# First chunk of a fused attention and two-FFN kernel: the sign of a weight piece ahead of its successor's rebase, head and rest one tick later, and the 1e-9 behind the exponentials

## Chip, core and metric

The kernel runs on one NeuronCore of one Trainium2 chip, in one launch. The metric is the device time in microseconds (us). TensorE is called PE in the profile, VectorE DVE, ScalarE ACT, GpSimd POOL, SyncE SP.

## What is computed

Three stages, each fed by the one before. Attention with 4 batches, 8 heads, 576 positions and head size 64; half of the heads see the last 32 positions, the other half every 32nd one. Then an FFN with h - tanh(h), then a gated FFN with silu. Everything is in fp32.

```python
scores = scale * np.matmul(q, k.transpose(0, 1, 3, 2))
scores = np.where(masks[None, :, :, :], scores, -1000000000.0)
scores = scores - np.max(scores, axis=-1, keepdims=True)
attn = np.exp(scores)
attn = attn / (np.sum(attn, axis=-1, keepdims=True) + 1e-09)
x = np.matmul(attn, v)                      # to (2304, 512)
h = x @ w_in                                # 512 -> 2048
x = (h - np.tanh(h)) @ w_out                # 2048 -> 512
g = x @ w_gate                              # 512 -> 1536
silu = g * (1.0 / (1.0 + np.exp(-g)))
out = silu * (x @ w_val) @ w_out2
```

## The kernel before

To keep fp32 precision, each matmul is made three times (`mm3`, L189 to L193) from operands that are split in two: a rounded high part and the remainder. So every weight must be split too. A weight comes in pieces of 128x512, read as 64-bit words, and a piece goes through eight steps (class `Piece`, L110 to L157):

- `load`: DMA from SyncE's queue into a staging buffer `st` (five of them, shared by all pieces)
- `high` (ScalarE, L124): the upper words without sign into a tile `m` (four tiles, used in turn); `low` (ScalarE, L127): the lower words scaled, in place
- `clamp` (VectorE, L130) and `shift` (VectorE, L134), together `rebase`: on `m`
- `join` (GpSimd, L142): adds the lower words to `m`
- `sign` (VectorE, L146): brings the sign from `st` into `m`; after it `st` is free
- `head` (ScalarE, L152): the rounded part of `m` into the weight tile `w`
- `rest` (GpSimd, L155): the remainder into `w`; `m` is free again. For eight of the 32 pieces, the streamed ones, `then` follows: a DMA from SyncE's queue that stores `w` for the later chunks.

The tokens are worked in five chunks. In the first one (c = 0, 512 tokens) the 32 weight pieces are made as they are needed. The first four are made during the attention of batch 0; the other 28 in the loop over f = 0 to 15 (16 slices of the hidden layer), two per iteration, by two calls of `feed1.tick()`. A tick is a stage of a pipeline over the pieces: tick t loads ahead, begins piece t, and goes on with the pieces begun in the ticks before it.

One iteration f of this loop issues, in this order: GpSimd's normalisation of the scores of attention group f-1 (`norm`: 1e-9 added on ScalarE at L290, reciprocal on VectorE at L294, multiplication on GpSimd at L296); the first part on TensorE (`first_part`, 12 matmuls into `ps_h`); tanh on ScalarE (L520) and h - tanh(h) on VectorE (L521); TensorE's product of group f-3 with the values; the first tick; TensorE's scores of group f (L265) and their masked maximum on VectorE (`top`, L273); the second part of f-1 on TensorE (12 matmuls into `ps_acc`); the transposes of group f-1 (L308) and their copy on VectorE (`bring`, L312); the split of the result (`parts`: L527 on ScalarE, L528 on VectorE); the exponentials of group f on ScalarE (L282), which also sum the rows; the second tick. There are twelve groups, so f = 13 to 15 have no scores and no normalisation. The first six groups are 80 columns wide (240 elements in the multiplication), the last six 96 (288).

Each engine works off its instructions in the order in which they are issued, and waits on semaphores for the others. There is no planner in this part: the order of the lines is the order on every engine. The first part at f needs piece 2f-1, the second part of f-1 needs piece 2f. From the second chunk on, the pieces are all there.

BV is 2. Batch 0's attention runs ahead of the loop; batch b = 1 runs in the first chunk, b = 2 and 3 in later ones.

Of the kernel before, what the change touches and what calls it, by code (L numbers as in the profile page):

```python
# [13 lines left out]
AF = mybir.ActivationFunctionType  # L14
# [19 lines left out]
BV = 2  # L34
# [39 lines left out]
def model_kernel(ctx: ExitStack, tc: tile.TileContext, q, k, v, mask, ident, sq, sk, sv, smask, w1, w2, out):  # L74
    nc = tc.nc
# [83 lines left out]
    class Feed:  # L159
# [18 lines left out]
        def tick(self):  # L178
            t = self.at
            self.at += 1  # L180
            self.load(t + 3)
            self.do(t, "high", "low")
            if t - 1 >= self.since:
                self.do(t - 1, "rebase", "join")
            if t - 2 >= self.since:
                self.do(t - 2, "sign", "head", "rest")

    def mm3(ps, w, c0, xh, xl, start, stop, goes_on=False):

# [5 lines left out]
    with tc.manual_schedule():  # L195
# [56 lines left out]
        class Group:  # L252
# [25 lines left out]
            def exp(self):  # L278
                w = self.w
                self.sm = att.tile([P, 16], F32, tag="sm", name="sm", bufs=3)[:, :GB]  # L280
                for i in range(GB):
                    nc.scalar.activation(  # L282
                        self.s[:, i, :w], self.s[:, i, :w], AF.Exp, scale=-1.0, bias=self.mx[:, i:i + 1],
                        **({"accum_out": self.sm[:, i:i + 1]} if self.b else {}),
                    )

            def norm(self, eng):
                w = self.w
                if self.b:
                    nc.scalar.activation(self.sm, self.sm, AF.Copy, bias=1e-9)  # L290
                else:
                    nc.vector.tensor_reduce(out=self.sm, in_=self.s[:, :, :w], axis=AX, op=ALU.add)
                    nc.vector.tensor_scalar(self.sm, self.sm, 1e-9, None, ALU.add)
                nc.vector.reciprocal(self.sm, self.sm)  # L294
                if eng is nc.gpsimd:
                    nc.gpsimd.tensor_tensor(  # L296
                        out=self.s[:, :, :w], in0=self.s[:, :, :w], in1=self.sm.unsqueeze(2).to_broadcast([P, GB, w]),
                        op=ALU.mult,
                    )
                    return  # L300
                for i in range(GB):
                    s, r = self.s[:, i, :w], self.sm[:, i:i + 1]
                    nc.scalar.mul(s, s, r)
# [214 lines left out]
        def bend(ps, n):  # L518
            t = epool.tile([P, CHUNK], F32, tag="e", name="t")
            nc.scalar.activation(t[:, :n], ps[:, :n], AF.Tanh)  # L520
            nc.vector.tensor_tensor(out=ps[:, :n], in0=ps[:, :n], in1=t[:, :n], op=ALU.subtract)  # L521
            return ps
# [492 lines left out]
        for c, (c0, n) in enumerate(CHUNKS1):  # L1015
# [10 lines left out]
            for f in range(NF1):  # L1026
# [26 lines left out]
                t = bend(ps, n)  # L1053
# [405 lines left out]
```

## Time and profile before

| | |
|---|---|
| median of 3 runs | 923.49 us |
| lowest, highest | 920.88, 923.81 us |
| the profiled execution | 920.19 us |
| its span, first to last instruction | 918.3 us |
| mean granted TensorE clock | 0.994 |
| TensorE busy in the span | 880.8 us (96%) |
| VectorE, ScalarE, GpSimd busy | 644.5, 458.7, 337.5 us |

A busy TensorE is not one at its peak, because matmuls are pipelined and their ends are modelled. The first chunk's loop runs from about 46 to 165 us of the span. In the rows further down a row of the timeline gives the start, the duration, the engine, the line, the operation and its tiles; in brackets stands how long the engine had been idle and what ended it. The end of an operation is its start plus its duration.

### The profile page before, as it was taken

What the parts mean: (1) busy time and instruction counts of PE and PEld (TensorE: products, weight loads), DVE (VectorE), ACT (ScalarE), POOL (GpSimd) and SP (SyncE); (2) the same over time, 40 slices, a digit from 0 to 9 for tenths busy, and PEclk for the clock granted to TensorE, in tenths of its full rate; (3) what the DMA queues carried; (4) which work ended last, traced back from release to release, by engine and by line L of the source; (5) the groups of instructions that cost most, each with busy time, mean ns of one, the idle gap of its engine ahead of it and who ended that gap; (6) DMA issues with size and microseconds to landing.
All of it is one profiled execution on the core that took longest, in us unless ns stands there. A gap on an engine that the chain in (4) does not pass through costs nothing. (4 is left out here: it accounts for less than half of the span.)

```text
span 918.3 us, 14160 instructions
## 1 busy us (share of the span) xinstructions
PE 880.8 (96%) x4918; PEld 722.3 (79%) x4918; DVE 644.5 (70%) x1222; ACT 458.7 (50%) x1034; POOL 337.5 (37%) x284
## 2 busy tenths in 40 slices
PE   8889998899999999999999988999999999999998
PEld 6567776777877778998887776888888887888888
DVE  6778786677776787326886785788877777966451
ACT  5577775534244523225555454555545446655431
POOL 2578887385526553001503421535544320000000
PEclk9899999999999999999999999999999999999999
DMA  8464743632343210426636642535452568968551
GB/s 272 154 195 155 255 158 113 241 110 82 103 140 118 69 46 24 146 85 237 221 92 205 207 149 82 183 117 165 154 184 87 200 216 291 344 229 278 198 202 42
DMA packets 66215, 150.38 MB, mean 164 GB/s; under 512 B 7200, under 2 KB 13344, under 8 KB 66144
## 3 DMA queue, kind: packets, MB, share of 16 engines
q1 hardware_dynamic: 65568, 149.04, 48.3%
q8 instruction: 39, 0.64, 0.3%
q10 hardware_dynamic: 576, 0.43, 0.2%
q14 instruction: 32, 0.26, 0.1%
HBM read 105.93 MB, written 43.52 MB: 163 GB/s over the span
## 5 line engine op out<-in xcount | busy, mean ns | idle before, releaser
L193 PE MATMUL ps_acc<-sl 128*128 128x512 f32 (+1 forms) x336 | 126.7, 377 | 5.0 <-DVE sl L738 5.0
L191 PE MATMUL ps_acc<-sl 128*128 128x512 f32 (+1 forms) x336 | 126.8, 377 | 3.4 <-ACT t L1206 3.4
L191 PE MATMUL ps_acc<-gl,w 128*128 128x512 f32 (+1 forms) x320 | 123.2, 385 | 3.4 <-DVE gl L528 3.3
L192 PE MATMUL ps_acc<-sl 128*128 128x512 f32 (+1 forms) x336 | 126.4, 376 | 0.0
L191 PE MATMUL ps_h<-xl,w 128*128 128x512 f32 (+1 forms) x320 | 121.1, 379 | 1.9 <-DVE gl L528 1.9
L193 PE MATMUL ps_h<-xh,w 128*128 128x512 f32 (+1 forms) x320 | 118.5, 370 | 0.7 <-POOL w L155 0.7
L193 PE MATMUL ps_acc<-gh,w 128*128 128x512 f32 (+1 forms) x320 | 118.5, 370 | 0.0
L192 PE MATMUL ps_acc<-gh,w 128*128 128x512 f32 (+1 forms) x320 | 118.3, 370 | 0.0
L192 PE MATMUL ps_h<-xh,w 128*128 128x512 f32 (+1 forms) x320 | 118.1, 369 | 0.0
L142 POOL TENSOR_TENSOR sl<-sl,st 128x512 int32<-128x512 int32 x36 | 52.0, 1450 | 164.6 <-DVE sl L134 134.2
L520 ACT ACTIVATE t<-ps_h 128x512 f32<-128x512 f32 (+1 forms) x80 | 44.0, 550 | 110.9 <-PE ps_h L193 110.9
L521 DVE TENSOR_TENSOR ps_h<-ps_h,t 128x512 f32<-128x512 f32 (+1 forms) x80 | 51.5, 643 | 65.5 <-ACT t L520 65.1
L976 DVE TENSOR_TENSOR sl<-sl 128x512 fp32r<-128x512 f32 (+1 forms) x120 | 73.9, 669 | 28.5 <-ACT sl L972 27.8
L528 DVE TENSOR_TENSOR gl<-ps_h,gh 128x512 fp32r<-128x512 f32 (+1 forms) x80 | 51.1, 638 | 39.5 <-ACT gh L527 38.0
L972 ACT CAST sl<-sl 128x512 fp32r<-128x512 f32 (+1 forms) x120 | 65.7, 599 | 25.2 <-DMA sl<-gd 19.0
L193 PEld LDWEIGHTS ps_acc<-sl 128*128 128x128 f32 x336 | 63.7, 190 | 17.2 <-DVE sl L738 5.9
L191 PEld LDWEIGHTS ps_acc<-sl 128*128 128x128 f32 x336 | 63.7, 190 | 16.8 <-ACT t L1206 5.5
L191 PEld LDWEIGHTS ps_acc<-gl,w 128*128 128x128 f32 x320 | 60.3, 188 | 18.5 <-DVE gl L528 6.0
L386 POOL TENSOR_TENSOR pr<-skv,sq 128x576 f32<-128x576 f32 (+8 forms) x40 | 56.3, 1437 | 50.2 <-DVE sc L393 30.6
L191 PE MATMUL ps_a<-sl 128*128 128x512 f32 (+1 forms) x192 | 70.3, 366 | 2.7 <-DVE t L1167 2.7
L192 PEld LDWEIGHTS ps_acc<-sl 128*128 128x128 f32 x336 | 63.6, 189 | 11.2
L193 PEld LDWEIGHTS ps_h<-xh,w 128*128 128x128 f32 x320 | 60.5, 189 | 11.8 <-POOL w L155 1.5
(125 smaller groups left out, 1960.9 us busy)
## 6 DMA issues: line engine op xcount, KB each, us to landing
st<-in_w SPq DMA_DIRECT2D x68, 512.0 KB, 4.7
gd<-t SPq DMA_DIRECT2D x84, 256.0 KB, 2.1
sl<-gd SPq DMA_DIRECT2D x84, 256.0 KB, 4.5
w<-w1s SPq DMA_DIRECT2D x32, 512.0 KB, 3.5
w3s<-sl SPq DMA_DIRECT2D x24, 256.0 KB, 4.0
sl<-w3s SPq DMA_DIRECT2D x24, 256.0 KB, 5.4
x2d<-o SPq DMA_DIRECT2D x18, 256.0 KB, 3.2
out_t<-t SPq DMA_DIRECT2D x18, 256.0 KB, 2.1
```

The lines of the kernel that those rows point to most:

```text
L142: nc.gpsimd.tensor_tensor(out=mi, in0=mi, in1=self.lo, op=ALU.add)
L191: nc.tensor.matmul(ps, lhsT=wh, rhs=xl, start=start, stop=False, skip_group_check=goes_on)
L192: nc.tensor.matmul(ps, lhsT=wh, rhs=xh, start=False, stop=False, skip_group_check=goes_on)
L193: nc.tensor.matmul(ps, lhsT=wl, rhs=xh, start=False, stop=stop, skip_group_check=goes_on)
L386: nc.gpsimd.tensor_tensor(out=t, in0=x, in1=y, op=ALU.mult)
L520: nc.scalar.activation(t[:, :n], ps[:, :n], AF.Tanh)
L521: nc.vector.tensor_tensor(out=ps[:, :n], in0=ps[:, :n], in1=t[:, :n], op=ALU.subtract)
L528: nc.vector.tensor_tensor(out=gl[:, :n], in0=t[:, :n], in1=gh[:, :n].bitcast(F32), op=ALU.subtract)
L972: nc.scalar.copy(got[0][:, 0, :n], got[0][:, 1, :n].bitcast(F32))
L976: nc.vector.tensor_tensor(out=w[:, 1, :n], in0=w[:, 1, :n].bitcast(F32), in1=w[:, 0, :n].bitcast(F32), op=ALU.subtract)
```

## The change

In `tick`, the order of the steps and the distance of two of them change. Before, tick t did `high` and `low` of piece t, `rebase` and `join` of t-1, then `sign`, `head` and `rest` of t-2. Now it does `head` and `rest` of t-3, `sign` of t-2, `high` and `low` of t, `rebase` and `join` of t-1. The first four pieces follow another table and are made as before.

For batch 1, whose groups run in the first chunk, the addition of 1e-9 to the row sums moves from `norm` to the end of `exp`. The batches 2 and 3 keep it in `norm`.

```diff
             t = self.at
             self.at += 1
             self.load(t + 3)
-            self.do(t, "high", "low")
-            if t - 1 >= self.since:
-                self.do(t - 1, "rebase", "join")
-            if t - 2 >= self.since:
-                self.do(t - 2, "sign", "head", "rest")
+            for back, *steps in ((3, "head", "rest"), (2, "sign"), (0, "high", "low"), (1, "rebase", "join")):
+                if t - back >= self.since:
+                    self.do(t - back, *steps)
...
+                if 0 < self.b < BV:
+                    nc.scalar.activation(self.sm, self.sm, AF.Copy, bias=1e-9)
 
             def norm(self, eng):
                 w = self.w
-                if self.b:
+                if self.b >= BV:
                     nc.scalar.activation(self.sm, self.sm, AF.Copy, bias=1e-9)
-                else:
+                if not self.b:
                     nc.vector.tensor_reduce(out=self.sm, in_=self.s[:, :, :w], axis=AX, op=ALU.add)
```

The lines from L184 to L284 stand up to two lines higher in the changed kernel: `mm3` is L189 to L191 there, `top` L271, the exponentials L280.

VectorE in the loop of the first chunk, from `gl` (the split of one iteration) to L521 of the next. Before (L130 and L134 are `clamp` and `shift`, L146 is `sign`):

```order
L528 TENSOR_TENSOR gl<-ps_h,gh 128x512
L130 TENSOR_SCALAR m<-m 128x512
L134 TENSOR_SCALAR m<-m 128x512
L146 SCALAR_TENSOR_TENSOR m<-st,m 128x512
L294 RECIPROCAL sm<-sm 128x3
L521 TENSOR_TENSOR ps_h<-ps_h,t 128x512
```

and now:

```order
L528 TENSOR_TENSOR gl<-ps_h,gh 128x512
L146 SCALAR_TENSOR_TENSOR m<-st,m 128x512
L130 TENSOR_SCALAR m<-m 128x512
L134 TENSOR_SCALAR m<-m 128x512
L294 RECIPROCAL sm<-sm 128x3
L521 TENSOR_TENSOR ps_h<-ps_h,t 128x512
```

`sign` has moved ahead of `clamp` and `shift`; the tick in the middle of the iteration shows the same.

ScalarE over the same place, from the split (L527) through the exponentials and the second tick to tanh (L520). L124 is `high`, L127 `low`, L152 `head`, w_1371 and w_1361 are weight tiles. Before:

```order
L527 CAST gh<-ps_h 128x512
L282 ACTIVATE s,sm<-s,mx 128x96 x3
L124 ACTIVATE m<-st 128x512
L127 ACTIVATE st<-st 128x512
L152 CAST w_1371<-m 128x512
L290 ACTIVATE sm<-sm 128x3
L520 ACTIVATE t<-ps_h 128x512
```

and now:

```order
L527 CAST gh<-ps_h 128x512
L280 ACTIVATE s,sm<-s,mx 128x96 x3
L285 ACTIVATE sm<-sm 128x3
L152 CAST w_1361<-m 128x512
L124 ACTIVATE m<-st 128x512
L127 ACTIVATE st<-st 128x512
L520 ACTIVATE t<-ps_h 128x512
```

`head` stands at the front of the tick, for the piece before, and the 1e-9 (L290, now L285) right behind the exponentials.

## Rows read from the trace of the kernel before

**Rows 1.** Waits of the whole run: engine line waited for: us in total, times, longest
```profile
ACT w L152 <- DVE m L146: 32.1, 27, 2.4
...
PE ps_a L308 <- POOL s L296: 7.4, 11, 1.5
```

**Rows 2.** Windows, first chunk and a later one: busy us (xinstructions), clock, DMA, GB/s
```profile
core 0: us, PE busy (x) PEld busy (x) DVE busy (x) ACT busy (x) POOL busy (x), PEclk, DMA share, GB/s
80.00:90.00 10.00, 9.47 (x79) 7.26 (x76) 7.68 (x20) 7.57 (x21) 8.06 (x6) 1.00 0.36 119
240.00:250.00 10.00, 10.00 (x45) 8.27 (x45) 6.59 (x9) 1.78 (x3) 8.41 (x6) 1.00 0.29 101
```

**Rows 3.** Timeline of ScalarE: the tanh of f=2 and f=12
```profile
58.30 0.58 ACT L520 ACTIVATE t<-ps_h 128x512 f32<-128x512 f32 x1
...
137.21 0.58 ACT L520 ACTIVATE t<-ps_h 128x512 f32<-128x512 f32 x1
```

**Rows 4.** Timeline of VectorE and GpSimd over one iteration
```profile
80.42 0.69 DVE L146 SCALAR_TENSOR_TENSOR m<-st,m 128x512 int32<-128x512 int32 x1
80.64 1.63 POOL L142 TENSOR_TENSOR m<-m,st 128x512 int32<-128x512 int32 x1 [0.88 <-POOL w L155]
82.23 1.30 POOL L155 TENSOR_TENSOR w<-m,w 128x512 fp32r<-128x512 f32 x1
82.38 0.70 DVE L521 TENSOR_TENSOR ps_h<-ps_h,t 128x512 f32<-128x512 f32 x1 [0.31 <-ACT t L520]
82.99 0.83 DVE L130 TENSOR_SCALAR m<-m 128x512 f32<-128x512 f32 x1
83.50 0.77 POOL L296 TENSOR_TENSOR s<-s,sm 128x240 f32<-128x240 f32 x1
83.86 0.69 DVE L134 TENSOR_SCALAR m<-m 128x512 int32<-128x512 int32 x1
84.47 0.68 DVE L146 SCALAR_TENSOR_TENSOR m<-st,m 128x512 int32<-128x512 int32 x1
84.68 1.65 POOL L142 TENSOR_TENSOR m<-m,st 128x512 int32<-128x512 int32 x1 [0.42 <-POOL s L296]
86.28 1.30 POOL L155 TENSOR_TENSOR w<-m,w 128x512 fp32r<-128x512 f32 x1
86.93 0.94 DVE L130 TENSOR_SCALAR m<-m 128x512 f32<-128x512 f32 x1
87.90 0.43 DVE L134 TENSOR_SCALAR m<-m 128x512 int32<-128x512 int32 x1
88.24 0.69 DVE L146 SCALAR_TENSOR_TENSOR m<-st,m 128x512 int32<-128x512 int32 x1
```

**Rows 5.** Timeline of ScalarE in the same iteration
```profile
81.14 0.62 ACT L152 CAST w<-m 128x512 fp32r<-128x512 f32 x1 [0.46 <-DVE m L146]
81.67 0.20 ACT L290 ACTIVATE sm<-sm 128x3 f32<-128x3 f32 x1
...
85.71 0.58 ACT L527 CAST gh<-ps_h 128x512 fp32r<-128x512 f32 x1
```

**Rows 6.** Timeline of VectorE and GpSimd before the steady part: pieces 1 to 5
```profile
26.72 1.29 POOL L142 TENSOR_TENSOR m<-m,st 128x512 int32<-128x512 int32 x1
27.96 0.67 POOL L296 TENSOR_TENSOR s<-s,sm 128x288 f32<-128x288 f32 x1
28.04 1.14 DVE L146 SCALAR_TENSOR_TENSOR m<-st,m 128x512 int32<-128x512 int32 x1 [1.83 <-POOL m L142]
...
51.94 0.59 POOL L296 TENSOR_TENSOR s<-s,sm 128x240 f32<-128x240 f32 x1
52.39 0.42 DVE L130 TENSOR_SCALAR m<-m 128x512 f32<-128x512 f32 x1
```

**Rows 7.** Timeline of GpSimd and TensorE at the first chunk's end
```profile
151.53 1.64 POOL L142 TENSOR_TENSOR m<-m,st 128x512 int32<-128x512 int32 x1 [0.88 <-POOL w L155]
155.28 1.64 POOL L142 TENSOR_TENSOR m<-m,st 128x512 int32<-128x512 int32 x1 [0.88 <-POOL w L155]
...
161.97 0.50 PE L191 MATMUL ps_acc<-gl,w 128*128 128x512 f32 x1 [1.22 <-DVE gl L528]
```

## The prediction

> **What bounds the kernel now.** I read the windows first. At 240 us, in a later chunk, TensorE is busy for all of the window; at 80 us, in the first, it is not [rows 2]. The change touches only the first chunk, and what it costs or gives there moves everything behind it by as much, since a TensorE that is always busy later has no slack to absorb it. Next come the starts of the tanh (L520), one per iteration f: 58.30 at f=2 and 137.21 at f=12 are ten iterations of 7.89 us [rows 3]. Behind them, without attention, one tick takes 3.75 us, from the end of one `join` (153.17) to that of the next (156.92) [rows 7]. The waits name ScalarE's `head` waiting for VectorE's `sign`, 32.1 us in all, and TensorE's transposes waiting for GpSimd's normalised scores [rows 1]. It looks as if the wait of `head` were the limit. The rows of one iteration say otherwise.
>
> Follow VectorE and GpSimd from 80.4 to 88.9 us [rows 4]. `clamp`, `shift` and `sign` on VectorE never make progress while a GpSimd instruction does. The `clamp` at 86.93 takes 0.94 us where a free one takes 0.42 [rows 4, 6], and it ends 0.29 after the `rest` beside it (87.58). The `join` at 84.68 takes 1.65 where a free one takes 1.29, and ends 1.18 after the `sign` beside it (85.15). The two engines take turns, one instruction at a time, and the one that waits goes next: the multiplication of the scores (L296, "mult") at 83.50 is issued behind `rest`, but the waiting `clamp` comes first. So one iteration is one chain of ends: `sign` 81.11, `join` 82.27, `rest` 83.53, `clamp` 83.82, mult 84.27, `shift` 84.55, `sign` 85.15, `join` 86.33, `rest` 87.58, `clamp` 87.87, `shift` 88.33, and `sign` again 88.93. That is 7.82 us, with hardly any time in which neither engine has the turn. This chain of turns is the bound; `head` waits beside it.
>
> The Trainium skill, "SBUF — State Buffer", section "Who interferes with whom", has a rule that speaks against this change: a VectorE instruction in a two-port mode, or with two SBUF inputs, and a GpSimd instruction that reads SBUF hold a shared port pair as a lock for the whole instruction. The trace agrees, with 0.94 for 0.42 us. If the engines only slowed each other in proportion, moving `head` could gain what its wait cost; that is the first rival below.
>
> **The change, part by part.** No piece gains or loses an instruction; they are ordered anew. (1) `head` and `rest` of a piece come one tick later, so that `head` finds its `sign` long done. The 32.1 us of ScalarE's wait [rows 1] go, but they are not on the chain of turns: worth 0 by themselves. (2) `sign` now stands ahead of `clamp` and `shift` on VectorE. This is what costs. `sign` of a piece needs the `join` of the tick before; `shift` now stands behind that `sign`, and the next `join` needs that `shift`. Before, `join` waited beside `sign` and took the turn the moment it ended; now `join`, `sign`, `clamp`, `shift` are a closed loop, each starting only when the last has handed on.
>
> The new iteration by its turns, each from the end of one to the end of the next:
> `rest` to a waiting `clamp` 0.29 (87.58 to 87.87); `shift` 0.46 (to 88.33); `join` 1.42 (it starts 0.13 after `shift`, as 84.55 to 84.68, and takes 1.29 free); `sign` 0.72 (starts 0.03 after `join`, as 28.01 to 28.04; takes 0.69); `clamp` 0.34 (VectorE starts its next 0.08 early, as 84.47; takes 0.42); the waiting `rest` 1.16 (as the `join` from 81.11 to 82.27; the two are equally long free); the waiting `shift` 0.28 (84.27 to 84.55); `join` 1.42; mult, queued right behind `join`, 0.54 (0.59 less an early start of 0.05); `sign` behind it 0.55 (28.63 to 29.18); the waiting `rest` 1.16 [rows 4, 6].
> The sum is 8.34 us. That mult goes ahead of `sign` is seen at 27.96 and 28.04 [rows 6]. For the 288-wide groups, mult takes 0.67 instead of 0.59, so 8.42; five narrow and six wide make a mean of 8.38.
>
> What the chain leaves out: the second `rest` of an iteration waits for a `head` that stands behind the exponentials. Were that `head` early, `rest` would go ahead of `sign`, and the tick would be 1.42 + 1.26 + 0.55 + 0.34 + 0.46 = 4.03 instead of 3.92: 8.5 in all. That pays for the upper bound. Without attention (f=13, 14) that order is the likely one, 4.03 per tick against 3.75.
>
> (3) The 1e-9 (0.20 us, seen at 81.67 [rows 5]) moves from the front of the iteration to behind the exponentials. VectorE's reciprocal no longer waits for it; it is then done before mult can have its turn, as the chain above assumes. Neither is a turn of its own. Its bounds are 0 and a gain of 2 us (0.2 in each of eleven iterations); I take 0.
>
> (4) Queues. The four `m` tiles: `high` of piece t needs `rest` of t-4, which now ends in the tick before instead of two before. By the chain above I estimate that it ends half a us ahead, so 0; were the cover gone, 0.1 to 0.3 in each iteration, 1 to 3 us. On SyncE the store of a streamed piece waits for its later `rest`, and the next loads stand behind it; the buffers of these loads still wait for the same `sign` one tick back, and the ticks are longer, so 0. TensorE's first part at f+1 needs the `rest` of the first tick of f. TensorE will now wait there rather than at the transposes; nothing on the chain of turns waits for that.
>
> The sum. Iterations f=2 to 12: 11 x (8.38 - 7.89) = +5.4. Four ticks behind them: 4 x (4.03 - 3.75) = +1.1. Start: the first `sign` (0.69, less 0.08) now stands ahead of a `clamp`, about +0.5. End: from the last `join` (156.92) to the first matmul of the last second part (161.97) it is 5.05 now [rows 7], through `sign`, `head`, tanh, L521, L527 and L528. After the change no tanh stands behind that `head`, as it does at 81.14 [rows 5]: `rest` 1.26, `sign` 0.55, then L521 0.62 (0.70 less 0.08) [rows 4], L527 0.61 (0.58 and a hand-over of 0.03) [rows 5], L528 as long as L521 with its hand-over, 0.73, and 0.05 to the matmul: 3.8 in all, -1.2. Together +5.8. The profiled execution (920.19, span 918.3) would become 926.0. It is 3.3 below the median of 923.49; on the median the forecast is 929.3.
>
> **The rivals.** *Faster, the wait of `head` was the limit.* For it: 32.1 us of waiting and a chain that also closes through ScalarE: `sign` ends 81.11, `head` starts 81.14, tanh follows, then L521 at 82.38 and `clamp` at 82.99 [rows 4, 5]. If GpSimd, now with `rest` ready early, ran one instruction behind VectorE so that no turn were lost, an iteration would cost its bare turns: 2 x (1.16 + 1.16 + 0.29 + 0.29 + 0.55) + 0.45 = 7.35, wide 7.43, mean 7.39: 11 x (7.39 - 7.89) = -5.5, so 918.0. It decides at whether `shift` ends before the `rest` of its tick begins. Against it: after `join` come `sign`, `clamp` and `shift` in any case, 0.72 + 0.34 + 0.46, and `rest` is waiting meanwhile.
> *No change.* The eleven hand-overs in the sum come from single rows. If they were 0.04 shorter each, an iteration would lose 0.4, and the total would be near +1; the gains at the end and the 1e-9 (up to 2) would bring it to zero: about 923.5.
> *Slower still.* `rest` ahead of `sign` in both ticks (8.60) adds 2.4, a wait for the `m` tiles up to 3: 931 to 934.
>
> **How the numbers follow.** The forecast with its harsher variant, slower, 0.80; no change 0.12; faster 0.08. A change of 0.3% (2.8 us) is about what a measurement can tell here. The forecast's own bounds are 926.5 (0.25 less per iteration) to 933. The range takes in the upper part of no change: 924 to 933.
>
> **What would show it.** In the changed kernel's rows: tanh starts 8.3 to 8.5 us apart from f=3 to f=12; `head`'s wait for `sign` nearly gone; one `clamp` in two lasting about 1.5 us, since it now waits for a whole `rest`, one `shift` in two about 1.4 and one `sign` in two 1.15; `join` short again, 1.3 us; TensorE's wait moved from L308 to the first part, released by `rest`. It would be wrong if `clamp` and `shift` run in 0.4 us beside GpSimd, if the spacing is below 7.8, or if the gap at the end of the chunk eats the sum.

## The result, and the profile after the change

The changed kernel takes 929.28 us in the median of 4 runs (928.46 to 929.33), the kernel before 922.74 in 4 runs beside it (920.88 to 923.81): ratio 1.0071, 95% interval 1.0052 to 1.0090. The change makes the kernel slower, by about what was forecast. The span of the profiled execution is 927.5 us against 918.3, the granted clock 0.993.

First the waits of the changed kernel over the whole run, to be held against [rows 1]; columns: engine and line waited for, us in total, times, longest.

```profile
ACT s L280 <- DVE mx L271: 32.2, 16, 3.0
...
DVE m L146 <- POOL m L142: 17.2, 20, 1.8
...
ACT w L152 <- DVE m L146: 9.2, 7, 2.0
...
PE ps_h L191 <- POOL w L155: 9.2, 13, 1.0
```

Those for the maximum, for `join` and for `rest` are in the kernel before:

```profile
ACT s L282 <- DVE mx L273: 6.2, 5, 1.7
...
DVE m L146 <- POOL m L142: 3.2, 3, 1.8
...
PE ps_h L193 <- POOL w L155: 0.7, 1, 0.7
```

The wait that the change is aimed at has gone from 32.1 to 9.2 us: `head` finds its `sign` done. In its place `sign` waits for `join` (17.2 us; 3.2 before), the exponentials wait for the masked maximum, which stands on VectorE behind the slower `clamp` and `shift` (32.2; 6.2 before), and TensorE's first part waits for `rest` (9.2; 0.7 before). The transposes' 7.4 us [rows 1] are down to 0.2. Waiting has moved, and the sum of these waits has grown.

The windows, as [rows 2]: TensorE's busy time in the first chunk's ten microseconds falls from 9.47 to 8.68, VectorE's rises from 7.68 to 9.07 though it has no more to do: the profile counts a held instruction as busy (the `clamp` of 1.50 us below, where a free one takes 0.42). In the later chunk TensorE is always busy, as before.

```profile
80.00:90.00 10.00, 8.68 (x56) 6.10 (x55) 9.07 (x19) 5.80 (x16) 7.17 (x6) 1.00 0.52 151
240.00:250.00 10.00, 10.00 (x55) 8.01 (x54) 8.62 (x11) 2.36 (x5) 2.52 (x4) 1.00 0.17 52
```

The starts of the tanh, ScalarE's timeline: f=0, f=2 and f=12 of the first chunk, and f=2 of the second. From f=2 to f=12 it is 84.44 us, 8.44 an iteration, against 7.89 [rows 3].

```profile
49.02 0.60 ACT L520 ACTIVATE t<-ps_h 128x512 f32<-128x512 f32 x1 [0.51 <-PE ps_h L191]
59.33 0.57 ACT L520 ACTIVATE t<-ps_h 128x512 f32<-128x512 f32 x1
143.77 0.57 ACT L520 ACTIVATE t<-ps_h 128x512 f32<-128x512 f32 x1
186.27 0.60 ACT L520 ACTIVATE t<-ps_h 128x512 f32<-128x512 f32 x1 [2.79 <-PE ps_h L191]
```

The same first and last mark in the kernel before:

```profile
46.83 0.59 ACT L520 ACTIVATE t<-ps_h 128x512 f32<-128x512 f32 x1
177.97 0.60 ACT L520 ACTIVATE t<-ps_h 128x512 f32<-128x512 f32 x1 [2.79 <-PE ps_h L193]
```

The first tanh comes 2.2 us later in the changed kernel, ahead of every instruction that the change touches. Over all kernels of this document, one trace of each, it lies between 46.8 and 50.7 us. So two traces are best compared by the distance between two marks. From the first tanh of the first chunk to the third of the second it is 131.14 us before and 137.25 after: +6.1. This **distance** is used for every kernel below.

One iteration of the changed kernel, VectorE first and then GpSimd, against [rows 4]:

```profile
83.03 0.69 DVE L146 SCALAR_TENSOR_TENSOR m<-st,m 128x512 int32<-128x512 int32 x1
83.64 0.42 DVE L130 TENSOR_SCALAR m<-m 128x512 f32<-128x512 f32 x1
84.10 1.40 DVE L134 TENSOR_SCALAR m<-m 128x512 int32<-128x512 int32 x1
85.42 0.16 DVE L294 RECIPROCAL sm<-sm 128x3 f32<-128x3 f32 x1
85.50 0.67 DVE L521 TENSOR_TENSOR ps_h<-ps_h,t 128x512 f32<-128x512 f32 x1
86.99 1.06 DVE L146 SCALAR_TENSOR_TENSOR m<-st,m 128x512 int32<-128x512 int32 x1 [0.82 <-POOL m L142]
87.97 1.50 DVE L130 TENSOR_SCALAR m<-m 128x512 f32<-128x512 f32 x1
89.51 0.43 DVE L134 TENSOR_SCALAR m<-m 128x512 int32<-128x512 int32 x1
...
91.41 0.69 DVE L146 SCALAR_TENSOR_TENSOR m<-st,m 128x512 int32<-128x512 int32 x1
```

```profile
81.69 1.31 POOL L142 TENSOR_TENSOR m<-m,st 128x512 int32<-128x512 int32 x1 [0.88 <-POOL w L155]
83.72 1.49 POOL L155 TENSOR_TENSOR w<-m,w 128x512 fp32r<-128x512 f32 x1 [0.72 <-DVE m L146]
85.63 1.33 POOL L142 TENSOR_TENSOR m<-m,st 128x512 int32<-128x512 int32 x1 [0.42 <-DVE sm L294]
86.91 0.59 POOL L296 TENSOR_TENSOR s<-s,sm 128x240 f32<-128x240 f32 x1
87.45 1.74 POOL L155 TENSOR_TENSOR w<-m,w 128x512 fp32r<-128x512 f32 x1
90.07 1.30 POOL L142 TENSOR_TENSOR m<-m,st 128x512 int32<-128x512 int32 x1 [0.88 <-POOL w L155]
```

This is the closed loop. `join` starts only when `shift` has ended (85.50 to 85.63, 89.94 to 90.07), `sign` when `join` has (83.00 to 83.03), and in between a `shift` of 1.40 or a `clamp` of 1.50 us has been held until `rest` had ended (it ends 0.29 and 0.28 us after it): a free `clamp` takes 0.42 [rows 6], a free `shift` 0.43. The bracket at 85.63 names the reciprocal, which happens to end between the two; the gap of 0.13 is the same at 90.07, without one. `join` itself is short again, 1.3 us where it took 1.65 beside `sign`.

At the chunk's end, where no attention is left, the timeline shows `join` and `rest` on GpSimd, `sign` on VectorE, the last `join`, and TensorE's first matmul of the last second part:

```profile
149.17 1.32 POOL L142 TENSOR_TENSOR m<-m,st 128x512 int32<-128x512 int32 x1 [0.88 <-POOL w L155]
...
154.48 1.27 POOL L155 TENSOR_TENSOR w<-m,w 128x512 fp32r<-128x512 f32 x1
154.56 1.74 DVE L146 SCALAR_TENSOR_TENSOR m<-st,m 128x512 int32<-128x512 int32 x1 [0.88 <-POOL m L142]
...
165.27 1.31 POOL L142 TENSOR_TENSOR m<-m,st 128x512 int32<-128x512 int32 x1 [1.48 <-issue]
170.36 0.50 PE L189 MATMUL ps_acc<-gl,w 128*128 128x512 f32 x1
```

Here `rest` goes ahead of `sign` in every tick, and `sign` takes 1.74 us. A tick is 4.02 us (149.17 to 165.27 is four of them) against 3.75 [rows 7]. From the end of the last `join` (166.58) to the matmul it is 3.78 us, where it was 5.05.

### The profile page after: what moved, and what is told of

It is laid out like the page before. It is cut to its first block, busy times and chain, and to the rows that moved or that the text cites. A ratio compares the mean times of both kernels' runs of the same rounds, so it can differ in the third digit from the quotient of the medians.

```text
span 927.5 us, 14179 instructions
## 1 busy us (share of the span) xinstructions
PE 886.2 (96%) x4918; PEld 722.2 (78%) x4918; DVE 657.8 (71%) x1222; ACT 460.1 (50%) x1034; POOL 334.1 (36%) x284
## 5 line engine op out<-in xcount | busy, mean ns | idle before, releaser
L191 PE MATMUL ps_acc<-sl 128*128 128x512 f32 (+1 forms) x336 | 126.9, 378 | 5.0 <-DVE sl L738 5.0
L189 PE MATMUL ps_acc<-sl 128*128 128x512 f32 (+1 forms) x336 | 127.1, 378 | 3.4 <-ACT t L1206 3.4
L191 PE MATMUL ps_h<-xh,w 128*128 128x512 f32 (+1 forms) x320 | 119.7, 374 | 9.2 <-POOL w L155 9.2
L189 PE MATMUL ps_acc<-gl,w 128*128 128x512 f32 (+1 forms) x320 | 122.8, 384 | 1.3 <-DVE gl L528 1.2
L191 PE MATMUL ps_acc<-gh,w 128*128 128x512 f32 (+1 forms) x320 | 119.6, 374 | 3.1 <-POOL w L155 2.4
L189 PE MATMUL ps_h<-xl,w 128*128 128x512 f32 (+1 forms) x320 | 121.1, 378 | 1.4 <-DVE gl L528 1.0
L520 ACT ACTIVATE t<-ps_h 128x512 f32<-128x512 f32 (+1 forms) x80 | 44.1, 551 | 115.2 <-PE ps_h L191 115.2
L521 DVE TENSOR_TENSOR ps_h<-ps_h,t 128x512 f32<-128x512 f32 (+1 forms) x80 | 51.1, 639 | 60.9 <-ACT t L520 60.5
L191 PEld LDWEIGHTS ps_h<-xh,w 128*128 128x128 f32 x320 | 60.6, 189 | 25.0 <-POOL w L155 15.0
L191 PEld LDWEIGHTS ps_acc<-sl 128*128 128x128 f32 x336 | 63.8, 190 | 17.4 <-DVE sl L738 5.9
L189 PEld LDWEIGHTS ps_acc<-sl 128*128 128x128 f32 x336 | 63.7, 190 | 16.3 <-ACT t L1206 5.1
L191 PEld LDWEIGHTS ps_acc<-gh,w 128*128 128x128 f32 x320 | 60.3, 188 | 19.0 <-POOL w L155 8.7
L189 PE MATMUL ps_a<-sl 128*128 128x512 f32 (+1 forms) x192 | 70.7, 368 | 2.7 <-DVE t L1167 2.7
```

The source lines that it names most:

```text
L189: nc.tensor.matmul(ps, lhsT=wh, rhs=xl, start=start, stop=False, skip_group_check=goes_on)
L191: nc.tensor.matmul(ps, lhsT=wl, rhs=xh, start=False, stop=stop, skip_group_check=goes_on)
```

## Experiments

The theory: `clamp`, `shift` and `sign` on VectorE and GpSimd's instructions take turns, one at a time, and the length of the chain of turns sets the pace of the first chunk. Rivals: the pace is set by how many ticks a step stands behind the one it needs (so the later `head` and `rest` are what counts); the moved 1e-9 is what costs; or VectorE's order costs by itself, whoever uses what at the same time.

Each kernel was timed in five rounds beside the kernel before. "Mean spacing" is that of the tanh from f=2 to f=12; the distance is compared with the 131.14 us of before. Single executions of the kernel before lay between 918.55 and 927.48 us in these rounds, so the medians are a coarse measure of a microsecond or two. The distance, though it comes from one trace of each kernel, is the finer one: the pairs whose loops should do the same (before and e4, e6 and e9, e7 and e10) agree in it to 0.3 us.

| kernel | median us | ratio, 95% interval | mean spacing us | distance, against before |
|---|---|---|---|---|
| changed | 929.28 | 1.0071 (1.0052 to 1.0090) | 8.44 | +6.1 |
| e1 | 919.99 | 0.9970 (0.9954 to 0.9987) | 7.95 | -1.4 |
| e2 | 931.55 | 1.0095 (1.0076 to 1.0113) | 8.53 | +8.6 |
| e3 | 930.68 | 1.0081 (1.0058 to 1.0103) | 8.55 | +7.5 |
| e4 | 923.70 | 1.0004 (0.9986 to 1.0021) | 7.89 | +0.2 |
| e5 | 921.06 | 0.9988 (0.9967 to 1.0008) | 7.98 | -1.1 |
| e6 | 923.67 | 1.0012 (0.9996 to 1.0028) | 7.59 | -4.1 |
| e7 | 928.13 | 1.0060 (1.0037 to 1.0083) | 7.78 | +0.5 |
| e8 | 924.60 | 1.0033 (1.0015 to 1.0051) | 7.90 | -1.7 |
| e9 | 918.44 | 0.9954 (0.9937 to 0.9971) | 7.56 | -4.4 |
| e10 | 921.78 | 0.9997 (0.9977 to 1.0016) | 7.78 | +0.2 |
| e11 | 915.24 | 0.9932 (0.9909 to 0.9955) | 7.47 | -6.4 |
| e12 | 918.58 | 0.9966 (0.9950 to 0.9982) | 7.71 | -3.5 |

**Which part of the change costs: e1 to e4.** e1 keeps the whole change and puts `sign` back behind `rebase` and `join`:

```diff
-            for back, *steps in ((3, "head", "rest"), (2, "sign"), (0, "high", "low"), (1, "rebase", "join")):
+            for back, *steps in ((3, "head", "rest"), (0, "high", "low"), (1, "rebase", "join"), (2, "sign")):
```

> The changed kernel with sign put back behind the rebase of the next piece; head and rest stay one tick later, the 1e-9 stays behind the exponentials. Theory of the turns (sign ahead of clamp and shift closes the loop join, sign, clamp, shift): the loss goes, tanh starts 7.9 to 8.0 us apart, the time within 2 us of the kernel before, ratio 0.998 to 1.002. Rival of the depth (the later rest, on which TensorE now waits, is what costs): the time stays near the changed kernel, ratio 1.005 to 1.008.

The loss is gone; e1 is even 0.3% below the kernel before, a little more than was expected. In the distance the gain lies at the two ends (1.1 us ahead of f=2, 0.9 behind f=12); the loop itself costs 0.06 us more per iteration than before. `head`'s wait for `sign` is down to 9.7 us in e1, as in the changed kernel, and the iteration is no shorter for it. The 32.1 us of [rows 1] were worth nothing in the loop.

e2 makes only the one move in the kernel before:

```diff
+            if t - 2 >= self.since:
+                self.do(t - 2, "sign")
             self.do(t, "high", "low")
...
-                self.do(t - 2, "sign", "head", "rest")
+                self.do(t - 2, "head", "rest")
```

> The kernel before with one thing changed: sign stands ahead of high, low, clamp and shift in its tick; head and rest stay in the same tick, at its end, and the 1e-9 stays where it was. Theory of the turns: all of the loss and a little more, because head is not gained: tanh starts 8.3 to 8.5 us apart, +6 to +8 us, ratio 1.0065 to 1.009. Rival of the depth: no loss, since nothing comes a tick later, ratio 0.998 to 1.002.

The whole loss is there, and 2.5 us more in the distance; it is a little above the range that was expected. Its timeline, VectorE and GpSimd, shows a `sign` that is caught behind a `rest`:

```profile
86.70 1.29 POOL L155 TENSOR_TENSOR w<-m,w 128x512 fp32r<-128x512 f32 x1
86.78 1.76 DVE L146 SCALAR_TENSOR_TENSOR m<-st,m 128x512 int32<-128x512 int32 x1 [0.32 <-POOL m L142]
...
91.13 1.29 POOL L155 TENSOR_TENSOR w<-m,w 128x512 fp32r<-128x512 f32 x1
91.20 1.77 DVE L146 SCALAR_TENSOR_TENSOR m<-st,m 128x512 int32<-128x512 int32 x1
```

Both times `rest` starts 0.07 to 0.08 us ahead of `sign`, and `sign` ends 0.55 after it. With a `rest` ready that early it goes ahead of `sign` in both ticks: the rival "slower still" of the prediction (8.60 an iteration, here 8.53). So the later `head` and `rest` of the change do not cost. By themselves they hardly gain either: e3 below, which is e2 with `head` and `rest` moved to the front of the next tick, has the same spacing (8.55) and is 1.0 us shorter in the distance.

e3 takes the 1e-9 back to `norm` in the changed kernel (first diff), e4 moves it alone in the kernel before (second diff).

```diff
-                if 0 < self.b < BV:
-                    nc.scalar.activation(self.sm, self.sm, AF.Copy, bias=1e-9)
...
-                if self.b >= BV:
+                if self.b:
```

```diff
+                if 0 < self.b < BV:
+                    nc.scalar.activation(self.sm, self.sm, AF.Copy, bias=1e-9)
...
-                if self.b:
+                if self.b >= BV:
```

> The changed kernel with the 1e-9 back in norm, in front of the iteration. Theory of the turns, by the prediction: 0 to 2 us slower than the changed kernel, tanh starts up to 0.15 us further apart than there; ratio to the kernel before 1.007 to 1.009. Rival (the moved 1e-9 delays head behind the exponentials and is part of the loss): faster than the changed kernel, ratio under 1.006.

> The kernel before with only the 1e-9 moved behind the exponentials of batch 1. Theory of the turns: it is no turn and not on the chain, so no change, ratio 0.999 to 1.001, the spacing of the tanh as before (7.8 to 7.9 us). Rival (the reciprocal's 0.79 us wait for it mattered): up to 5 us faster, ratio 0.995 to 0.997.

Alone it does nothing, spacing 7.89 to the hundredth. In the changed kernel it helps: e3, which takes it back, is 0.11 us per iteration slower and 1.4 us longer in the distance, which the ratios do not separate (1.0081 and 1.0071).

**A `clamp` that takes no turn: e6, e7, then e9, e10.** The wait was to be taken from one operation without changing the order. The Trainium skill, "SBUF — State Buffer", section "Who interferes with whom", excepts one form of `tensor_scalar` from those that can enter the two-port modes: the one that also writes out its accumulator. So `clamp`, from the fifth piece on, also writes row sums that nothing reads. e6 is the kernel before with this, e7 the changed kernel.

```diff
+    junk = const.tile([P, 4], F32, name="junk")[:, :1]
...
-            nc.vector.tensor_scalar(self.m, self.m, HI_LEAST, HI_MOST, ALU.max, ALU.min)
+            kw = {"accum_out": junk} if self.summed else {}
+            nc.vector.tensor_scalar(self.m, self.m, HI_LEAST, HI_MOST, ALU.max, ALU.min, **kw)
```

> The kernel before, with one addition: from the fifth piece on, clamp also writes its row sums into an unused 128x1 tile. By the Trainium skill (SBUF - State Buffer, section Who interferes with whom) the form with an accumulator is not in the mode that takes the shared port. Theory of turns: clamp then needs no turn; alone it gets longer (0.42 to about 0.7 us), yet beside a rest it ends without waiting for it. Two turns of each iteration go, spacing of the tanh 7.4 instead of 7.89: about 5 us less, ratio 0.9945, between 0.992 and 0.998. Rival (no turns, clamp is simply slowed in proportion or the chain runs through head): each clamp adds some 0.28 us on VectorE, twice in eleven iterations: +6 us, ratio 1.006, or 1.000 where VectorE has the slack. If clamp still ends with GpSimd's instruction, 1.2 to 1.5 us long, the accumulator does not keep it out of the turns, and the ratio is 1.000 to 1.006 too.

> The changed kernel with the same addition: from the fifth piece on, clamp also writes its row sums into an unused tile. Theory of turns: the clamp that waited 1.5 us for a whole rest no longer does, the loop of join, sign, clamp, shift gets shorter by most of that wait, tanh 7.7 to 7.8 us apart instead of 8.38: about 5.5 us less than the changed kernel, ratio to the kernel before 1.0005, between 0.998 and 1.003. Rival (the loss is only the order in which VectorE must work, whoever uses the ports): clamp's extra 0.28 us stands in that loop twice an iteration, +6 us on the changed kernel: ratio to the kernel before 1.010 to 1.014.

Both totals missed: 1.0012 where 0.9945 was expected, 1.0060 for 1.0005. The first chunk did not: the distance is -4.1 and +0.5, near what the theory wanted. By the medians about 5 us were lost behind it in each. TensorE's timeline in a later chunk tells where: ten matmuls of e6 take 2.33 us from start to start.

```profile
253.21 0.40 PE L198 MATMUL ps_h<-xh,w 128*128 128x512 f32 x1
...
255.54 0.40 PE L196 MATMUL ps_acc<-gl,w 128*128 128x512 f32 x1
```

The only part of the edit that can reach there is the new 16-byte tile (per partition), which was laid ahead of the weights and stages. e9 and e10 write the row sums into a column of `pad`, a tile that is there already and otherwise unused:

```diff
-    junk = const.tile([P, 4], F32, name="junk")[:, :1]
...
-    ctx.enter_context(tc.tile_pool(name="pad", bufs=1, side="right")).tile([P, 24], F32, name="pad")
+    junk = ctx.enter_context(tc.tile_pool(name="pad", bufs=1, side="right")).tile([P, 24], F32, name="pad")[:, :1]
```

> As e6_clamp_sum_before, but the unused row sums go into a tile that is there already (pad), so that no other tile moves; in e6 the new 16-byte tile moved weights and stages by 16 bytes, and the matmuls of the later chunks stood 0.233 us apart instead of 0.229. Theory of turns, with the addresses as the cause of what ate the gain: clamp 0.67 us in every case, tanh 7.38 to 7.46 us apart as in e6, and the later chunks as long as before: 3 to 4 us less than the kernel before, ratio 0.996, between 0.993 and 0.999. Rival (the addresses do not matter; the loss behind the first chunk comes from the accumulator itself): ratio 1.001 again.

> As e7_clamp_sum_after, with the row sums in the pad tile. Theory of turns: the change's own order, with a clamp that takes no turn: tanh 7.7 to 7.85 us apart, 5.5 us less than the changed kernel; ratio to the kernel before 1.001, between 0.998 and 1.003. Rival (the order costs 6 us whoever uses the ports, or the accumulator costs by itself): 1.006 or more, as e7.

Now both totals follow the theory: 0.9954 and 0.9997. Ten matmuls of e9 at the same place take 2.27 us:

```profile
253.12 0.39 PE L194 MATMUL ps_acc<-gl,w 128*128 128x512 f32 x1
...
255.39 0.39 PE L195 MATMUL ps_h<-xh,w 128*128 128x512 f32 x1
```

The claim about `clamp` itself is read from VectorE's groups of operations on the `m` tiles, 50 to 160 us (duration in ns, least, median, most). In the kernel before:

```profile
L130 DVE TENSOR_SCALAR m<-m x28: 412/870/945, 49.7 to 153.8; 128x512 f32<-128x512 f32 x28
```

and in e9:

```profile
L133 DVE TENSOR_SCALAR_CACHE_REDUCE m<-m x28: 672/676/678, 51.9 to 151.9; 128x512 f32<-128x512 f32 x28
L133 DVE DVE_READ_ACCUMULATOR m<-m x28: 79/83/85, 52.5 to 152.5; 128x1 f32 x28
```

The plain `clamp` takes 0.41 to 0.95 us, as GpSimd lets it; the one with row sums 0.67 to 0.68 all 28 times, whatever stands beside it. The exception that the Trainium skill states holds here. A `clamp` that does more work, is longer when free and is followed by an extra instruction of 0.08 us makes the kernel 0.46% faster. In e10, the changed order, the same is seen in one place, VectorE and GpSimd:

```profile
84.75 1.74 POOL L158 TENSOR_TENSOR w<-m,w 128x512 fp32r<-128x512 f32 x1
85.27 0.67 DVE L133 TENSOR_SCALAR_CACHE_REDUCE m<-m 128x512 f32<-128x512 f32 x1
...
85.98 0.79 DVE L137 TENSOR_SCALAR m<-m 128x512 int32<-128x512 int32 x1
```

`clamp` begins and ends inside `rest` (84.75 to 86.49); the `shift` behind it is still held, to 0.28 after `rest`. With `clamp` out of the turns the loop is 7.78 us an iteration instead of 8.44, in the very order that cost 0.55. This refutes the rival that the order costs by itself.

**A better order: e5, e8, e11, e12.** If the turns are what counts, `rebase` and `join` should stand so that `join` does not wait for `sign`'s turn and `shift`'s both. e5 is the kernel before with `rebase` and `join` in the tick of `high`; e8 adds the row sums of e6 to it.

```diff
-            self.do(t, "high", "low")
+            self.do(t, "high", "low", "rebase", "join")
             if t - 1 >= self.since:
-                self.do(t - 1, "rebase", "join")
+                self.do(t - 1, "sign")
             if t - 2 >= self.since:
-                self.do(t - 2, "sign", "head", "rest")
+                self.do(t - 2, "head", "rest")
```

> Tick t does high, low, rebase and join of t, then sign of t-1, then head and rest of t-2; the 1e-9 stays in norm. Nothing is taken away, the order alone differs. Theory (VectorE's clamp, shift and sign and each GpSimd instruction take turns): with clamp, shift and join at the front of the tick, join no longer closes a loop with sign; a waiting engine takes the turn the moment the other ends. The tanh stand 7.6 to 7.8 us apart instead of 7.89, the first chunk ends about 3 us earlier: ratio 0.9965, between 0.994 and 0.999. Rival (no turns; what counts is how far a step stands behind the one that it waits for): clamp now waits for high and low of its own tick, two ScalarE operations of some 0.6 us each, and join for it: each tick gets longer by up to 0.5 us, 26 ticks: ratio 1.003 to 1.012.

> The order of the kernel with rebase in the same tick, with clamp's row sums added as in the two runs before. Theory of turns: both gains add in part, the iteration is then near TensorE's own work in it: tanh 7.35 to 7.5 us apart, 5 to 6 us less than the kernel before, ratio 0.9935, between 0.991 and 0.996; below the kernel with rebase in the same tick alone. Rival (no turns): clamp's extra 0.28 us twice an iteration makes it slower than that kernel by up to 6 us.

e5 gave 0.9988, which is not to be told from no change, and its spacing missed: 7.98 where 7.6 to 7.8 was expected. e8 gave 1.0033, a miss, of which some 5 us are the tile's place, if it costs here what it costs in e6 and e7. The rest is in the spacing: in e5 7.08 us in some iterations, 9.88 in the one from f=7 (11.05 in e8). SyncE's and ScalarE's timeline of e5 at the long one:

```profile
94.18 0.33 SPq L459 DMA_DIRECT2D w1s<-w  x1
...
96.50 1.64 SPq L118 DMA_DIRECT2D st<-in_w  x3
...
103.12 0.66 ACT L124 ACTIVATE m<-st 128x512 f32<-128x512 f32 x1 [3.88 <-DMA st<-in_w]
```

Three loads leave together behind the store of a streamed piece (and three K, Q and V loads between), and `high` waits 3.88 us for one of them. The iteration from f=7 has such a wait in the kernel before and in e9 too, where it is the longest of the ten (8.20 and 8.58 us); the nine others of e9 have a mean of 7.45, as was expected of all. ScalarE's timeline of the kernel before, and of e9:

```profile
100.48 0.68 ACT L124 ACTIVATE m<-st 128x512 f32<-128x512 f32 x1 [2.28 <-DMA st<-in_w]
```

```profile
101.08 0.67 ACT L126 ACTIVATE m<-st 128x512 f32<-128x512 f32 x1 [2.50 <-DMA st<-in_w]
```

e12 issues load t+4 right behind `sign` of t-1, so that one more load is out ahead of each such store; e11 is e12 with the row sums in `pad`.

```diff
-            self.load(t + 3)
             self.do(t, "high", "low", "rebase", "join")
             if t - 1 >= self.since:
                 self.do(t - 1, "sign")
+            self.load(t + 4)
```

> As e8_clamp_sum_best with the row sums in the pad tile, and with the load of piece t+4 issued right behind sign of t-1, ahead of the rest and store of t-2, instead of load t+3 at the front of the tick. In e5 and e8 two or three loads left SyncE together at 96.5 us, behind a store that waited for its rest and a load that waited for TensorE, and ScalarE then waited 3.9 us for a weight. If the place behind the store is the cause, that wait goes: 3 to 5 us less than e8 and the addresses' 4 us besides, ratio 0.993, between 0.990 and 0.996. If the load that waits for TensorE is, the wait stays: ratio 0.997 to 1.000.

> As e11_load_ahead without the row sums: the order of e5, load t+4 right behind sign, clamp in its plain form. It parts the two gains of e11. Theory of turns: the long gaps of e5 at f=3, 8 and 9 go (they were waits for a load), the plain clamp takes its turns again: tanh 7.6 to 7.75 us apart in the mean over f=2 to 12 instead of 7.47 in e11; 2 to 3 us less than the kernel before, ratio 0.997, between 0.995 and 0.9985, and e11 below it by 2 to 3 us. Rival (the whole gain of e11 is the load): as e11, 0.993.

Neither has a wait of `high` for a load any more in the loop. e12 takes 7.71 us per iteration and 0.9966 of the time, e11 7.47 and 0.9932, both inside what was expected; the order with its earlier load is worth 3.5 us in the distance (127.63) and the freed `clamp` 2.8 more (124.79). How much of the 3.5 the earlier load would give in the kernel before, with the old order, was not tried. e11 is 0.7% below the kernel before and, by the two ratios, 1.4% below the changed one. What bounds it now was not settled.

## Why the prediction was right

**The bound.** That `clamp`, `shift` and `sign` take turns with GpSimd was read from single rows; e9 and e10 show it by taking one of them out. The `head` wait as the limit, the first rival, falls with e1.

**The chain.** From the end of one `join` (83.00) to the end of the next but one (91.37) the changed kernel shows, with the forecast in brackets: `sign` 0.72 (0.72), `clamp` 0.34 (0.34), `rest` 1.15 (1.16), `shift` 0.29 (0.28), `join` 1.46 (1.42), the multiplication 0.54 (0.54), `sign` 0.55 (0.55), `rest` 1.14 (1.16), `clamp` 0.28 (0.29), `shift` 0.47 (0.46), `join` 1.43 (1.42). Sum 8.37 against 8.34: the order of the turns came as forecast, and the hand-overs taken from rows of before carry over to 0.04 us.

**The sum.** It is taken from end to end of `join`, pieces counted from 0. GpSimd's timeline has pieces 4, 5 and 27 in the kernel before:

```profile
50.67 1.31 POOL L142 TENSOR_TENSOR m<-m,st 128x512 int32<-128x512 int32 x1 [2.39 <-ACT s L282]
...
53.51 1.54 POOL L142 TENSOR_TENSOR m<-m,st 128x512 int32<-128x512 int32 x1 [0.98 <-DVE m L134]
...
140.19 1.65 POOL L142 TENSOR_TENSOR m<-m,st 128x512 int32<-128x512 int32 x1 [0.42 <-POOL s L296]
```

and pieces 4 and 5 in the changed one (27 and 31 are shown above, at 149.17 and 165.27):

```profile
52.85 1.32 POOL L142 TENSOR_TENSOR m<-m,st 128x512 int32<-128x512 int32 x1 [2.98 <-DVE sm L294]
...
56.44 1.31 POOL L142 TENSOR_TENSOR m<-m,st 128x512 int32<-128x512 int32 x1 [1.72 <-DVE mx L271]
```

| stretch, end of `join` to end of `join` | before | after | measured | forecast |
|---|---|---|---|---|
| start: piece 4 to piece 5 | 3.07 | 3.58 | +0.5 | +0.5 |
| eleven iterations: piece 5 to 27 | 86.79 | 92.74 | +5.95 | +5.4 |
| four ticks: piece 27 to 31 | 15.08 | 16.09 | +1.0 | +1.1 |
| end: to the last second part | 5.05 | 3.78 | -1.3 | -1.2 |
| sum | | | +6.2 | +5.8 |

The medians differ by 6.5 us. That the forecast of 929.3 meets 929.28 to the hundredth is luck: it added 5.8 us to a median of 923.49, and the runs beside the changed kernel had one of 922.74. The term that was too small is the iteration, by 0.05 us: 8.43 where 8.38 was taken, since the iterations with wide groups take 8.44 to 8.48 where 8.42 was worked out, and the one from f=2 takes 8.64. The spans differ by more, 9.2, mostly because the profiled execution of the changed kernel was 2.2 us late at the first tanh already.

**The 1e-9** at 0 was right by itself (e4). In the new order it saves 0.11 us per iteration (e3): without it ahead of `head`, `rest` comes early enough to go ahead of `clamp` in both ticks (in e3 it starts at 90.31 and `clamp` at 90.47, where the changed kernel has 83.72 and 83.64). It lies within the bounds that the prediction gave it, a gain of up to 2 us. The wait for an `m` tile, taken at 0 as well, is there once in the changed kernel, for 0.5 us.

**What it did not say:** that the exponentials would wait 32.2 us for the maximum, behind the held `clamp` and `shift` on VectorE. It cost nothing that shows in the sum: the chain of turns is as long as forecast without it.

## What to carry to other kernels

Where two engines exclude one another, a long wait in the list of waits can be worth nothing: write down the ends of the operations of both engines in one order, and count how often the path passes from one to the other and what each hand-over costs. Moving an operation so that it needs the other engine's result and is needed by its next one closes a loop, which here cost more than the wait that stood beside it. Then look for a form of the operation that takes no turn, even a longer one, and test such an edit with nothing else moved, buffers included.

## What was not expected of the hardware

**Where a tile lies changes TensorE's pace.** e6 and e9 differ only in where an unused row sum is kept, and so in whether a new 16-byte tile stands ahead of weights and stages. Between 220 and 320 us, matmuls of 128x512 that start within 0.3 us of the one before them stand on average 0.233 us apart in the three kernels with the new tile (e6, e7, e8) and 0.228 to 0.229 in the eleven others; the granted clock is 1.00 there in e6 and in e9. From the third tanh of the second chunk to the last tanh of all it is 323.2 to 323.6 us in the three, and 319.0 to 320.8 in the others. By the medians the whole kernel is 0.6% longer (e6 against e9, e7 against e10), nearly as much as the change under study; of these 5 to 6 us the traces place 3.1 and 4.1 in that stretch, and where the rest is was not found. Which tile's place does it, and whether the granularity is 16 bytes, was not tried.
